# One fused core program, 832 operations: another order on every queue, the same operations

## The chip, the core and the metric

The program runs on one NeuronCore of a Trainium2 chip. Five engines have instruction queues of their own and work through them strictly in order: TensorE (PE in the profile, its weight loads PEld), VectorE (DVE), ScalarE (ACT), GpSimd (POOL) and SyncE (SP, which here issues nearly all DMAs). They wait for one another through semaphores. The metric is the device time of the program in microseconds (us), lower is better. Time before: 160.24 us, the median of 3 runs (159.95 to 160.32).

## The reference

Two independent computations share the core, and their results stand side by side in the output (2048 rows, 576 + 576 columns).

```python
# A: gated long convolution (S = 2048, D = 576, 4 taps)
k_shift = sum over t of k_pad[:, t:t+S, :] * shift_k[:, ks-1-t]
kv = k_shift * v
y  = irfft(rfft(kv padded to 2S) * rfft(ssm_k padded to 2S))[:S]   # per channel
a  = q * (bf16(y) + kv * ssm_D)
# B: linear attention, 32 heads of 18
q, k, v = split(x @ wqkv);  phi(t) = where(t > 0, t + 1, exp(t)) + 1e-6
kv  = einsum("bhsd,bhse->bhde", phi(k), v);  z = sum_s phi(k)
o   = (phi(q) @ kv) / (phi(q) . z + 1e-6)
b   = o @ wo
return concat([a, b], axis=-1)
```

## The kernel before

The kernel first records 832 operations in a list (`Prog.op`): each has the buffers that it reads and writes and the engines that may run it. Nothing in that list says in which order they run. `_issue` reads the order from two tables of numbers at the end of the file. `PLAN` is a list of tokens such as `P391` or `D142`: the letter gives the engine (P TensorE, D VectorE, A ScalarE, G GpSimd, S SyncE), the number the operation. The tokens of one letter, read from left to right, are that engine's queue. `PLACES` gives each buffer its address in SBUF or its bank in PSUM. Where a new buffer lies on an older one, its first writer waits for the older one's last users.

Part A is a Fourier convolution in two steps, since n = 16a + b:

- the taps (L402, `tap`; L236, `tap+` and `tapv`) make kv from k and v on VectorE and GpSimd, in six pieces (three ranges of 192 channels, two halves of b);
- L436 transposes the filter, and L467 (`s1h` for the filter, `s1u` for kv) multiplies by a table over a; ScalarE or VectorE moves each result from PSUM to SBUF as `Ch` or `Cu` (L229 and L231 are the helper's lines for such copies);
- VectorE transposes in blocks of 32 (L506), and L515 (`s2h`, `s2u`) does the 16-point step. There are nine pieces of 64 channels, 0 to 8, for the filter and again for kv. Each piece has four L515 operations, one for each quarter of 32 partitions of TensorE's array; they have consecutive tokens, so P391, P393, P395, P397 are quarters 0 to 3 of the filter's piece 0. Each consists of four matmuls of 32x32;
- for each piece two products (L236, `p1` and `p2`) combine the spectra, `p2` with `X`, a copy whose real and imaginary rows DMAs have swapped; L551 (`i1`) and L576 (`i2`) transform back, and the result is multiplied with q and stored.

Part B projects x (L623 k, L644 q; ScalarE takes the exponential, VectorE makes phi), forms G = x^T phi(k) (L673), then kv and M = kv wo (L708, L770), scales phi(q) with the reciprocal denominators (L236, `pqT`), and multiplies with M (L813, `out`), 16 row groups of two halves each, stored from `ob`.

The first part of x is loaded in two pieces (`x_sb0`), transposed by TensorE (L323) and copied to `xT0`; the other three parts come through transposing loads (L345, L347). While x is on its way, nine matmuls on a constant tile (`cft`, L844) keep TensorE at work. Small loads: `srow` holds the four taps' weights, which ScalarE rearranges to `srt`, a DMA writes to `w_scr`, and another reads back broadcast as `Wj`. A manual dependency (`two`) makes a GpSimd product wait for the VectorE product that stands before it in the table; nothing makes a VectorE product wait for a GpSimd one.

SP's DMAs use eight semaphores in turn, so each DMA is issued only when the one eight places before it has landed.

Of the kernel before, what the change touches and what calls it, by code (L numbers as in the profile page):

```python
# [874 lines left out]
S60 S25 P149 P143 D142 D439 P98 D139 S51 A396 G42 A150 P469 A144 P400 A410 P406 P402 D151 D145 A99 A401 P446 A403
G471 D448 A407 S50 P164 A165 S46 S472 P146 P453 D470 D100 A447 P451 S45 P440 G52 D166 P449 D457 A147 P158 A441 D148
P404 A450 P411 A452 D64 A412 P464 A454 G47 P460 P152 A465 A461 P455 P444 A405 P413 A159 A414 S38 A456 D160 P155
A445 P194 D72 P442 P462 P458 S43 P415 A416 S224 P185 D65 A463 A153 D154 A459 P475 A186 A476 A195 P161 P191 A443
P170 A192 D187 D196 A156 P167 A39 A168 A162 G66 D157 D193 S61 S48 P179 A180 P473 P134 S225 D169 S647 A474 D163 P104
P128 D73 S223 A171 G44 A135 D136 D74 A105 D106 A129 S626 S668 D181 D172 P122 A123 P107 G75 G477 D130 A49 A108 P173  # L880
P113 D124 A114 P125 A126 P182 A183 D109 D80 S646 A174 P119 G67 D127 D115 D184 A120 P131 P101 A132 D121 S62 A102
D133 P110 P116 S226 D81 P176 S17 A111 D112 A117 A177 P188 D103 G82 D118 D175 P217 A189 D178 S625 P220 D83 A218 A219
A221 P488 D190 P480 S63 P486 A489 D68 P230 D231 A481 P197 D232 P490 S667 A487 A198 A199 D76 P237 P233 P492 P202
D234 A491 S547 A493 D238 P478 A203 A479 G69 A204 D77 P482 D239 G78 P200 S253 D235 D236 D70 A483 A201 P484 S254 A485
# [5 lines left out]
S588 P693 G251 P319 S252 G249 D320 P691 A694 P339 P679 A686 D616 A692 P683 A684 A340 P344 P356 A357 P506 D680 P580  # L890
D345 P619 D658 P510 D716 P540 A507 P565 A581 A566 P617 S242 G243 P346 A541 P354 P321 A355 A620 D511 A322 P349 P341
P519 A350 P665 P623 P501 D347 A618 P515 D737 D342 P661 S22 P329 A520 D516 P336 D330 P334 A624 A666 P659 P508 P638
D502 A662 A337 P642 D335 P644 P517 D509 P621 P304 S343 P311 D622 A639 A518 A305 A643 A660 A312 P351 A352 D645 P324
P561 S348 A325 S705 S338 P544 P640 P738 P742 P723 A562 D695 P663 P281 A664 A641 P284 A724 D739 D743 A282 S746 P294
# [60 lines left out]
```

## Time and profile before

| | |
|---|---|
| median of 3 runs | 160.24 us |
| span of the profiled execution, first to last instruction | 158.3 us |
| what lies around the span | 1.9 us (160.24 - 158.3) |
| PE busy | 149.8 us, 95% |
| DVE busy | 141.8 us, 90% |
| ACT busy | 125.1 us, 79% |
| POOL busy | 59.6 us, 38% |
| SP's hardware queue, share of 16 DMA engines | 66.6% |

The profiled execution's own device time is not given beside its span; the 1.9 us around it is taken as the same for both kernels. Busy times are of one execution. The profile counts only instructions that compute as busy, and a matmul's end is modelled. The chain of waits is followed back from the last instruction, so it shows one path among several that are nearly as long.

### The profile page before, as it was taken

Reading aid. Unit: us, or ns where it says so; the run is one execution under the profiler, and the core shown is the slowest. Engines: PE = TensorE matmul, PEld = TensorE weight load, DVE = VectorE, ACT = ScalarE, POOL = GpSimd, SP = SyncE. Lnnn points to the kernel's source line nnn. Section 1 sums busy time; section 2 is a strip of 40 time slices with the busy share of each in tenths; the row PEclk is TensorE's granted clock in tenths of the full one; section 3 lists DMA queues with packets and bytes.
Section 4 is the critical chain, followed back from the end, with each engine's and each line's share of the span. In section 5 each row is a group of like instructions: output and inputs, shape, how many; then the busy total and the mean of one; then the engine's idle time right before and its main releaser. Section 6 shows DMA issues by size and latency. Waiting matters only on the chain.

```text
span 158.3 us, 4158 instructions
## 1 busy us (share of the span) xinstructions
PE 149.8 (95%) x1663; PEld 118.6 (75%) x1663; DVE 141.8 (90%) x170; ACT 125.1 (79%) x229; POOL 59.6 (38%) x53
## 2 busy tenths in 40 slices
PE   6899999999999999999999999999999999999960
PEld 2478885535679888788888887877767799999960
DVE  1547999999999998999999999999989999999690
ACT  4038999999996566467559699999899999998760
POOL 8801310011163554603611999799290000001520
PEclk9999999999999999999999999999999999999997
DMA  5999939999999809965546867881463599405766
GB/s 146 283 384 313 245 79 299 284 187 239 352 384 259 299 15 333 377 270 103 99 131 214 159 149 209 312 288 63 178 232 112 173 331 361 143 4 147 188 181 160
DMA packets 26317, 34.37 MB, mean 217 GB/s; under 512 B 15802, under 2 KB 20923, under 8 KB 25530
## 3 DMA queue, kind: packets, MB, share of 16 engines
q1 hardware_dynamic: 25754, 32.54, 66.6%
q0 software_dynamic: 544, 1.57, 5.6%
q8 instruction: 13, 0.21, 0.7%
q14 instruction: 6, 0.05, 0.1%
HBM read 20.86 MB, written 4.99 MB: 163 GB/s over the span
## 4 chain that ended last, share of the span: by engine, by line
PE 78%; ACT 8%; DVE 6%; DMA 2%; issue 1%; SPq 1%; DVEq 0%; ACTq 0%
PE ps_all L813 13%; PE ps_all L623 12%; PE ps_all L673 12%; PE ps_all L644 11%; PE ps_all L467 8%; PE ps_all L551 8%; PE ps_all L515 5%; ACT sph L229 3%; PE ps_all L576 3%; ACT V L229 3%; DMA x_sb<-in_B_x_dram 2%; PE ps_all L436 2%; DVE Ch L231 2%; ACT yb L229 1%; PE ps_all L708 1%
## 5 line engine op out<-in xcount | busy, mean ns | idle before, releaser
L644 PE MATMUL ps_all<-xT,wq 128*126 128x512 bf16 (+1 forms) x100 | 23.8, 381 | 0.1
L813 PE MATMUL ps_all<-M,pqT 126*128 126x288 bf16 (+1 forms) x160 | 22.5, 287 | 0.0
L623 PE MATMUL ps_all<-wk,xT 128*128 128x288 bf16 x160 | 20.4, 286 | 0.4 <-DVE xT L231 0.4
L402 DVE TENSOR_TENSOR m<-kh,Wj 128x6144 bf16<-128x6144 bf16 x6 | 20.1, 3349 | 0.0
L229 ACT ACTIVATE Cu<-ps_all 128x768 bf16<-128x768 f32 x22 | 17.3, 856 | 3.2 <-PE ps_all L467 3.2
L623 PEld LDWEIGHTS <-xT 128*128 128x128 bf16 x160 | 17.4, 110 | 3.1 <-DVE xT L231 0.6
L236 POOL TENSOR_TENSOR pqT<-pqT,rb 126x1024 bf16<-126x1024 bf16 (+1 forms) x9 | 19.1, 2174 | 1.0 <-DVE v L236 1.0
L813 PEld LDWEIGHTS <-pqT 126*128 126x128 bf16 (+1 forms) x160 | 16.6, 110 | 3.7 <-issue 1.9
L644 PEld LDWEIGHTS <-wq 128*126 128x126 bf16 (+1 forms) x100 | 12.5, 131 | 8.7 <-issue 2.2
L229 ACT ACTIVATE V<-ps_all 128x512 bf16<-128x512 f32 x32 | 17.2, 624 | 1.8 <-PE ps_all L551 1.8
L628 ACT ACTIVATE ek<-ps_all,neg 128x576 bf16<-128x576 f32 x16 | 11.9, 743 | 8.3 <-PE ps_all L623 8.3
L467 PEld LDWEIGHTS <-Gsb 128*128 128x128 bf16 x192 | 16.1, 98 | 2.6 <-issue 1.6
L551 PE MATMUL ps_all<-Esb,sph 128*128 128x128 bf16 x144 | 17.9, 219 | 0.1
L551 PE MATMUL ps_all<-Esb,X 128*128 128x128 bf16 x144 | 17.9, 219 | 0.0
L236 POOL TENSOR_TENSOR m<-m 128x1536 bf16<-128x1536 bf16 x4 | 12.4, 3096 | 13.1 <-DVE m L236 8.9
L673 PE MATMUL ps_all<-pk,x_sb 128*128 128x289 bf16 (+1 forms) x128 | 17.1, 287 | 0.0
L229 ACT ACTIVATE sph<-ps_all 128x512 bf16<-128x512 f32 x30 | 16.6, 608 | 0.2
L229 ACT ACTIVATE Ch<-ps_all 128x768 bf16<-128x768 f32 x19 | 15.2, 853 | 1.0 <-PE ps_all L467 0.8
L229 ACT ACTIVATE spu<-ps_all 128x512 bf16<-128x512 f32 x28 | 15.1, 613 | 0.6 <-PE ps_all L515 0.6
L236 POOL TENSOR_TENSOR q<-yb,q 128x384 bf16<-128x384 bf16 x4 | 3.6, 912 | 29.4 <-DVE yb L231 27.6
L673 PEld LDWEIGHTS <-x_sb 128*128 128x128 bf16 x128 | 12.3, 98 | 2.9
L551 PEld LDWEIGHTS <-sph 128*128 128x128 bf16 x144 | 14.0, 98 | 0.5 <-DVE sph L236 0.2
(96 smaller groups left out, 301.9 us busy)
## 6 DMA issues: line engine op xcount, KB each, us to landing
X<-sph SPq DMA_DIRECT2D x18, 256.0 KB
v<-in_A_v_dram SPq DMA_DIRECT2D x2, 1152.0 KB
out_dram<-ob SPq DMA_DIRECT2D x16, 144.0 KB
q<-in_A_q_dram SPq DMA_DIRECT2D x1, 2304.0 KB
out_dram<-q SPq DMA_DIRECT2D x12, 192.0 KB
rb<-r_scr SPq DMA_DIRECT2D x8, 252.0 KB
x_sb<-in_B_x_dram SPq DMA_DIRECT2D x3, 576.0 KB
kh<-in_A_k_dram SPq DMA_DIRECT2D x1, 1584.0 KB
```

The costliest lines, as they stand in the source:

```text
L229: nc.scalar.activation(out=o, in_=i, func=ACTF.Copy)
L236: return (nc.vector if e == "DVE" else nc.gpsimd).tensor_tensor(out=o, in0=a, in1=b, op=op)
L402: return nc.vector.tensor_tensor(out=m.t[:], in0=i0, in1=i1, op=ALU.mult)
L467: nc.tensor.matmul(ps.t[:, bank, lo - 384 * bank:hi - 384 * bank], lhsT=Gsb.t[:, b, ri, :], rhs=src[:, lo - CC * j:hi - CC * j], start=Tru ...
L515: nc.tensor.matmul(ps.t[32 * j:32 * j + 32, 0, :], lhsT=W2()[32 * kh:32 * kh + 32, :], rhs=ct.t[32 * kh:32 * kh + 32, 8 * j:8 * j + 8], st ...
L551: nc.tensor.matmul(ps.t[:, 0, 128 * c:128 * c + 128], lhsT=src.t[:, 4 * hh + c, :], rhs=Esb.t[:, 32 + wi, :], start=(wi == 0), stop=(wi == 1))
L576: nc.tensor.matmul(ps.t[:, 0, n * j:n * j + n], lhsT=Esb.t[:, 2 * b + ri, :], rhs=V[gi].t[:, 2 * b + ri, :], start=(ri == 0), stop=(ri == 1))
L623: nc.tensor.matmul(ps.t[:, hh, 0:HALF], lhsT=cols(xT.t[0:KT[t], t, :], r), rhs=wk.t[0:KT[t], t, HALF * hh:HALF * hh + HALF], start=(t == 0 ...
L628: P.op("A", lambda e: nc.scalar.activation(out=eb.t[:], in_=ps.t[:, :, 0:HALF], func=ACTF.Exp, bias=neg1.t[:]), rd=[ps, neg1], wr=[eb], na ...
L644: nc.tensor.matmul(ps.t[0:hn, 0, :], lhsT=wq.t[0:KT[t], t, h0:h0 + hn], rhs=xT.t[0:KT[t], t, :], start=(t == 0), stop=(t == 4))
L673: nc.tensor.matmul(ps.t[0:m, 0, 0:n], lhsT=x4[r // 4].t[:, r % 4, :] if t == 4 else x_sb[r // 4].t[:, r % 4, 128 * t:128 * t + 128], rhs=p ...
L813: nc.tensor.matmul(ps.t[:, 0, 0:HALF], lhsT=cols(pqT[r // 8].t[0:kn, c, 512 * (r // 4 % 2):512 * (r // 4 % 2) + 512], r), rhs=M.t[0:kn, c, ...
```

## The change

No operation is added or removed. `PLAN` and `PLACES` hold other numbers: other orders on all five queues, and 83 operations of 832 go to another engine. The diff is those two tables and nothing else; three of the 36 lines of `PLAN` show its kind (the first line, one in the first run of L515, and the last).

```diff
--- before.py
+++ after.py
 PLAN = """
-G0 G6 D830 P831 G10 S28 A15 S16 G222 S26 G12 G14 G5 P30 D27 G57 P32 D33 A29 G9 G7 D31 S54 P36 A37 S53 G1 G2 S21 P34
...
-D408 P140 A434 A468 P431 P425 S41 P137 P391 D432 P395 A426 P393 P397 D399 A141 S58 S24 A392 P409 D398 A394 S40 A138
...
-D762 S769 P772 A773 S763 P770 A771 D774 S775
+D830 P831 G5 G10 S26 S16 G0 G1 G2 D27 G12 P30 D31 S28 S54 S53 G222 G6 G29 P32 A33 P36 D37 P34 P89 D35 A90 D91 S359 S21
...
+P140 A424 P425 A426 D439 S41 A141 P137 A138 P391 A392 D142 S58 P395 P397 G42 S51 D139 S40 D457 S60 G8 P409 A410 G7 A15
...
+A767 P764 A765 D768 P758 A759 S781 P760 A761 D762 P770 A771 P772 A773 S769 P314 S763 A315 D774 S775 S318
```

Three places on which the working rests follow, as the queues stand in the built programs.

**The start.** ScalarE's first rows before: `warm` is an exponential of one element, `x40` a copy of a strip of x, `srt` the rearranged tap weights.

```order
L283 ACT_TABLE_LOAD
L283 ACTIVATE warm_6_76<-neg1_1_57 128x1
L229 ACTIVATE x40_11_87<-x_sb0_5_74 128x2x64
L229 ACTIVATE xT0_13_102<-ps_all 128x256
L628 ACTIVATE ek_19_141<-ps_all,neg1_1_57 128x576
L628 ACTIVATE ek_20_154<-ps_all,neg1_1_57 128x576
L628 ACTIVATE ek_21_174<-ps_all,neg1_1_57 128x576
L229 ACTIVATE hT0_22_177<-ps_all 128x8x128
L229 ACTIVATE hT0_22_177<-ps_all 128x8x64
L229 ACTIVATE Ch_29_228<-ps_all 128x4x96x2 x4
L229 ACTIVATE Ch_33_294<-ps_all 128x4x96x2
L229 ACTIVATE srt_34_298<-srow_31_255 64x36
```

ScalarE's first rows after:

```order
L229 ACT_TABLE_LOAD
L229 ACTIVATE xT0_9_92<-ps_all 128x256
L628 ACTIVATE ek_12_127<-ps_all,neg1_6_76 128x576
L628 ACTIVATE ek_16_146<-ps_all,neg1_6_76 128x576
L229 ACTIVATE srt_17_148<-srow_15_134 64x36
L628 ACTIVATE ek_19_171<-ps_all,neg1_6_76 128x576
L229 ACTIVATE hT0_18_169<-ps_all 128x8x64
L229 ACTIVATE hT1_21_203<-ps_all 128x8x64 x2
L229 ACTIVATE Ch_23_213<-ps_all 128x4x96x2 x6
```

`srt` moved from behind five evictions of `Ch` to before the third exponential; `x40` went to GpSimd, and the large eviction of `hT0` (128x8x128) to VectorE. On SP the rows that follow from it, before:

```order
L222 DMA srow_31_255<-in_A_shift_k_dram 64x36
L222 DMA wq_25_184<-in_B_wqkv_dram 64x576
L222 DMA wq_25_184<-in_B_wqkv_dram 128x4x576
L222 DMA kh0_12_98<-in_A_k_dram 15x1728
L347 DMA_TRANSPOSE xT1_39_356<-in_B_x_dram 128x1x512
L222 DMA kh0_12_98<-in_A_k_dram 112x1728
L222 DMA w_scr<-srt_34_298 64x4x9
L345 DMA_TRANSPOSE xT1_39_356<-in_B_x_dram 128x4x512
L222 DMA kh0_12_98<-in_A_k_dram 128x4608
L222 DMA Wj_44_399<-w_scr 128x2304
L347 DMA_TRANSPOSE xT3_46_425<-in_B_x_dram 128x1x512
```

and after:

```order
L222 DMA kh0_29_296<-in_A_k_dram 15x1728
L222 DMA hs_31_301<-in_A_ssm_k_dram 96x2048
L222 DMA wq_26_244<-in_B_wqkv_dram 128x4x576
L222 DMA w_scr<-srt_17_148 64x4x9
L222 DMA wq_26_244<-in_B_wqkv_dram 64x576
L347 DMA_TRANSPOSE xT1_37_354<-in_B_x_dram 128x1x512
L222 DMA kh0_29_296<-in_A_k_dram 112x1728
L347 DMA_TRANSPOSE xT3_42_383<-in_B_x_dram 128x1x512
L345 DMA_TRANSPOSE xT1_37_354<-in_B_x_dram 128x4x512
L222 DMA kh0_29_296<-in_A_k_dram 128x4608
L222 DMA wv5_10_97<-in_B_wqkv_dram 64x576
L222 DMA Wj_57_506<-w_scr 128x2304
```

`w_scr`, which waits for `srt`, moved ahead of all transposing loads, and `srow` (13th DMA before) is now the 8th. A small load of `kh0` (k with its halo) stands ahead of the two first transposing loads.

**GpSimd's last products**, before (`rb` are the reciprocal denominators, `spu` and `sph` the spectra of kv and of the filter):

```order
L236 TENSOR_TENSOR pqT0_36_332<-pqT0_36_332,rb_137_1442 126x1024
L236 TENSOR_TENSOR pqT0_36_332<-pqT0_36_332,rb_149_1556 126x1024
L236 TENSOR_TENSOR X_82_735<-spu_151_1577,X_82_735 128x2048
L236 TENSOR_TENSOR q_175_2003<-yb_183_2294,q_175_2003 128x2x192
L236 TENSOR_TENSOR q_175_2003<-yb_185_2323,q_175_2003 128x2x192
L236 TENSOR_TENSOR q_175_2003<-yb_184_2303,q_175_2003 128x2x192
L236 TENSOR_TENSOR q_175_2003<-yb_186_2397,q_175_2003 128x2x192
```

and after:

```order
L236 TENSOR_TENSOR pqT0_41_371<-pqT0_41_371,rb_131_1440 126x1024
L236 TENSOR_TENSOR pqT0_41_371<-pqT0_41_371,rb_139_1501 126x1024
L236 TENSOR_TENSOR X_147_1567<-spu_143_1535,X_147_1567 128x2048
L236 TENSOR_TENSOR sph_54_466<-spu_143_1535,sph_54_466 128x2048
L236 TENSOR_TENSOR q_180_2151<-yb_177_2123,q_180_2151 128x4x192
L236 TENSOR_TENSOR q_180_2151<-yb_184_2271,q_180_2151 128x2x192
L236 TENSOR_TENSOR q_180_2151<-yb_186_2388,q_180_2151 128x2x192
```

Both products of piece 3 now stand on GpSimd, one behind the other; before, VectorE made the one into `sph`.

**The end**, on SP before:

```order
L222 DMA out_0_dram<-ob_176_2072 128x576
L222 DMA out_0_dram<-q_175_2003 128x4x192 x2
L222 DMA out_0_dram<-ob_174_2000 128x576
L222 DMA out_0_dram<-q_175_2003 128x4x192 x5
L222 DMA out_0_dram<-ob_161_1718 128x576
L222 DMA out_0_dram<-q_175_2003 128x4x192 x5
```

and after:

```order
L222 DMA out_0_dram<-q_180_2151 128x4x192 x2
L222 DMA out_0_dram<-ob_156_1693 128x576
L222 DMA out_0_dram<-q_180_2151 128x4x192 x4
L222 DMA out_0_dram<-ob_157_1701 128x576
L222 DMA out_0_dram<-q_180_2151 128x4x192 x5
L222 DMA out_0_dram<-ob_175_2042 128x576
```

A store of `ob` now is the very last DMA; the five matmuls that feed its second half (P314) moved from the middle of the last stage to behind the last `i2`.

More of the change, by code (lines that the diff above doesn't have):

```diff
@@ L875 @@
[L875 to L884, printed above, removed]
@@ L890 @@
[L890 to L894, printed above, removed]
@@ new lines @@
+P140 A424 P425 A426 D439 S41 A141 P137 A138 P391 A392 D142 S58 P395 P397 G42 S51 D139 S40 D457 S60 G8 P409 A410 G7 A15
+P393 A394 P143 A144 D145 P149 A150 D448 A396 P98 A99 D100 G13 D151 G57 G52 P146 A398 A147 D148 P404 D405 P406 A407
+P442 A443 P164 P451 A165 D166 P446 P453 P400 S224 A454 A401 A452 P469 D470 S25 D64 A447 P158 P444 P449 A159 D160 A450
+D72 A445 P464 P402 A403 P152 P155 A465 P455 A456 P413 A414 P440 A441 S50 P185 P462 A463 S46 G47 P411 A412 G471 A156
+D157 P458 A459 P191 A192 S45 P415 D65 G66 P460 A461 A416 A153 D154 P194 P161 A162 D163 A195 D196 D193 S472 S48 A186
@@ new lines @@
+P488 P212 A213 D70 D71 A489 S223 P490 A491 S255 P207 D84 G85 S263 P492 A493 A214 P202 A203 D494 D512 A208 D503 A209
+P521 A522 S252 P531 A532 A204 P200 A201 S226 P533 P525 P535 A526 A536 A534 P215 P523 A524 P527 P529 A528 A530 D579
+D537 A216 P205 A206 P614 A615 P610 P604 A605 A611 P210 A211 G262 G260 S244 P600 D256 A601 P687 A688 P689 A690 D264
+P499 A500 D558 P513 D514 P227 D228 D229 P612 A613 P608 D609 P602 A603 P267 D268 G266 P275 A276 P269 P271 S257 G258
+A272 D270 P273 D274 P582 P504 A505 P497 P495 A583 P606 D498 A607 A496 G86 D87 P277 D278 P679 P681 A680 A682 S265 S246
@@ new lines @@
+P685 A686 P344 A345 P339 A340 P691 A692 P693 D616 D658 P683 D684 A694 P319 P356 A357 D320 P506 A507 D637 S242 S250
+P580 A581 P565 P540 S248 P510 D511 P617 A541 P619 A618 P349 A350 A620 P354 D566 D355 P321 D322 P341 A342 S646 S625
+P665 A666 S668 G251 G249 D737 P515 P623 P621 P661 P659 D660 D624 P519 A662 A516 A622 G245 G247 P336 A337 P346 A520
+D347 G243 P334 A335 P329 A330 S626 G627 S589 G628 P517 P561 A562 P644 D716 P642 A643 D518 P638 P501 D502 P508 P351
+D352 A645 P304 A509 D305 A639 P324 A325 P311 A312 S647 S567 P719 D695 P723 D720 P663 A664 P738 P740 D741 P544 A545
@@ new lines @@
+P742 A743 P281 A282 S22 P294 A295 D724 D739 P284 A285 P542 D543 P696 P702 A697 P640 D641 S705 P721 D722 D649 S704 S358
+S747 S343 S338 S588 P538 P331 P286 D648 S547 A539 A703 A332 P289 A287 P717 A290 P563 S667 D669 P698 P744 A699 P559
+A718 A745 D670 P700 A701 D707 P629 S546 P635 A636 P309 S726 S288 S746 P633 A634 P296 A297 P631 S348 A564 A630 P306
+P656 A307 P650 A657 P671 D632 D706 A560 S725 D728 P675 D727 P677 S353 A676 P279 P673 D672 A678 A310 S313 A651 P652
+A674 P710 A653 D749 P586 P584 A587 D711 A585 D590 P316 P708 A317 P735 A280 A736 P654 A655 A709 P714 P731 D748 P712
```

31 lines of the change are left out of this document (13 added, 18 removed), and 32 rows, old and new, of the table PLACES.

## The prediction

> **What bounds the kernel now.** I read the busy shares first, then the busy time by stage.
>
> ```profile
> span 158.3 us, 4158 instructions
> PE 149.8 (95%) x1663; PEld 118.6 (75%) x1663; DVE 141.8 (90%) x170; ACT 125.1 (79%) x229; POOL 59.6 (38%) x53
> ...
> core 0: us, PE busy (x) PEld busy (x) DVE busy (x) ACT busy (x) POOL busy (x), PEclk, DMA share, GB/s
> 8.20:24.20 16.00, 15.55 (x160) 13.11 (x160) 12.85 (x19) 12.89 (x19) 2.98 (x7) 1.00 0.89 250
> 24.20:45.00 20.80, 20.74 (x191) 11.55 (x191) 20.80 (x22) 20.54 (x40) 3.22 (x3) 1.00 1.09 285
> ...
> 105.00:124.40 19.40, 19.40 (x277) 13.33 (x276) 18.17 (x27) 18.31 (x44) 10.58 (x5) 1.00 0.46 172
> 124.40:136.00 11.60, 11.60 (x178) 11.20 (x177) 11.60 (x12) 11.00 (x25) 0.00 (x0) 1.00 0.78 284
> 136.00:151.00 15.00, 14.92 (x223) 14.56 (x221) 13.33 (x21) 12.97 (x29) 3.22 (x4) 1.00 0.42 119
> ```
>
> PE is busy nearly all the time from 8.2 to 151 us, at a granted clock of 1.00. It isn't alone: from 24.2 to 45 DVE (20.80 of 20.80) and ACT (20.54) are full as well, and from 105 to 136 all three nearly are. So an order can gain in three ways only: a shorter start, less PE time for the same matmuls, and a shorter end. Everything it gains on PE must also be kept up with by the engines that empty PSUM. Where I say that something comes at a time "by its queue", I have added the durations that stand ahead of it on its engine in the new order, and looked up when that engine had done the same amount of work before. The sum is made against the profiled execution: 158.3 us of span and 1.9 us around it, which together are the median of 160.24.
>
> **The start.** Next I read the timeline of the first 20 us, and SP's waits.
>
> ```profile
> 3.63 0.31 ACT L229 ACTIVATE x<-x_sb 128x128 bf16<-128x128 bf16 x1 [1.39 <-DMA x_sb<-in_B_x_dram]
> 5.43 1.37 DVE L231 COPY x<-x_sb 128x128 bf16<-128x128 bf16 x1 [4.02 <-DMA x_sb<-in_B_x_dram]
> 8.06 0.49 SPq L222 DMA_DIRECT2D srow<-in_A_shift_k_dram  x1
> 8.20 3.85 PE L623 MATMUL ps_all<-wk,xT 128*128 128x288 bf16 x30 [0.43 <-DVE xT L231]
> 13.08 1.02 ACT L229 ACTIVATE hT<-ps_all 128x1024 bf16<-128x1024 bf16 x1 [0.25 <-PE ps_all L436]
> 14.16 1.48 PE L467 MATMUL ps_all<-hT,Gsb 128*128 128x192 bf16 x16
> 18.95 0.22 ACT L229 ACTIVATE srt<-srow 64x36 bf16<-64x36 bf16 x1
> 19.19 0.69 SPq L222 DMA_DIRECT2D w_scr<-srt  x1
> 19.92 3.63 SPq L345 DMA_TRANSPOSE xT<-in_B_x_dram  x1
> ...
> SPq L222 <- DMA wk<-in_B_wqkv_dram: 0.5, 1, 0.5
> ...
> L231 DVE COPY hT<-ps_all 128x1024 bf16<-128x1024 bf16 x3 | 1.9, 677 | 0.0
> ```
>
> The first k projection (L623) starts at 8.20, after a chain: the piece of x that is needed first is loaded third, its strip copy on DVE takes 1.37 us, and PE, evictions and L623 follow. The two pieces change places (S26 first, S28 third). The piece loaded first landed by 3.63, when ACT copied its strip; so the DVE copy now runs from about 3.6 to 5.0, under the nine matmuls on the constant tile. The other strip is on POOL, behind memsets that are done before it lands at 5.4. From the landing at 5.43 the rest of the chain takes 8.20 - 5.43 - 1.37 = 1.4 us, so evictions would allow L623 at about 6.9. But it needs wk too, and wk is at the same place in SP's queue: SP waited for its landing and issued `srow` at 8.06. Its landing just under 8.0 is the new limit, and I take 0.2 us. Ends: 0, if wk lands later beside other traffic, and 1.3 (8.20 - 6.9), if earlier.
>
> At 14.16 the first L467 waited for the eviction of `hT` on ACT (13.08 + 1.02 = 14.10). This eviction is now DVE's, which takes 0.68 for such a copy (the row below), and ACT and DVE then work on the two halves at once. The wait of some 0.3 goes: 0.3 us, from 0 to 0.5.
>
> SP stood still from 14.26 to 19.19, because `srt` was made on ACT at 18.95 only. It is now made in ACT's slot before the third exponential, near 11.5, once `srow`, now 8th, has landed. All later loads move up by 2 to 3 us. I cost this at 0: no PE row before waits for one of them. What hides them is the work of 24 to 45 us; the transposing loads stay one behind the other on this queue, only earlier.
>
> **L515 on PE.** The chain of waits has 12 of the 15 runs of L515 as steps of their own. Four of them:
>
> ```profile
> 28.82 0.55 PE ps_all L515 x16
> 93.15 0.34 PE ps_all L515 x8
> 105.36 0.90 PE ps_all L515 x24
> 112.42 0.99 PE ps_all L515 x28
> ```
>
> The run at 93.15 holds two operations on different quarters of the array, and takes 0.34. The run at 28.82 (P400 P406 P402 P446, quarters 0, 3, 1, 3) has one quarter twice, and takes 0.55. The run at 112.42 has quarter 2 four times: 0.99. So a run costs about 0.34, and 0.21 more for each time that its commonest quarter is repeated; operations on other quarters cost nothing. Counted from the tokens, before there are 15 runs with 18 repeats: 15 x 0.34 + 18 x 0.21 = 8.9 us. After there are 16 runs with 11 repeats: 5.4 + 2.3 = 7.7 us. PE saves 1.1 us (about 0.5 before 45 us, 0.6 after 93).
>
> [...]
>
> Between 0 and 1.1 I take half, 0.55, since DVE and ACT are full beside it but shed some work themselves:
>
> ```profile
> L231 DVE CAST V<-ps_all 128x512 bf16<-128x512 f32 x4 | 2.7, 683 | 0.1
> L231 DVE CAST spu<-ps_all 128x512 bf16<-128x512 f32 x8 | 5.2, 685 | 1.0 <-PE ps_all L515 1.0
> L236 DVE TENSOR_TENSOR pqT<-pqT,rb 126x1024 bf16<-126x1024 bf16 x1 | 0.7, 684 | 0.0
> L686 DVE TENSOR_SCALAR GT<-ps_all,gcol 128x288 bf16<-128x288 f32 x2 | 0.9, 475 | 0.0
> L231 DVE CAST ob<-ps_all 128x288 bf16<-128x288 f32 x10 | 4.5, 447 | 1.3 <-PE ps_all L813 1.1
> L231 DVE CAST yb<-ps_all 128x384 bf16<-128x384 f32 x6 | 3.3, 553 | 0.3 <-ACT yb L229 0.2
> L231 DVE CAST Ch<-ps_all 128x768 bf16<-128x768 f32 x5 | 4.6, 962 | 0.7 <-ACT Ch L229 0.7
> L236 DVE TENSOR_TENSOR sph<-spu,sph 128x2048 bf16<-128x2048 bf16 x9 | 10.8, 1215 | 0.0
> ```
>
> DVE's net exchange: it gains 4 evictions of V (2.7), 2 of spu (1.4) and one `pqT` product (0.7), together 4.8; it gives up 2 of GT (0.95), 3 of ob (1.3), 3 of yb (1.7), one of Ch (1.0) and one `sph` product (1.2), together 6.1. Three evictions of hT of 512 elements are exchanged for 1024, 768 and 512: 768 elements more, at 677 / 1024 ns each an estimate of 0.5. Net -0.8 us. ACT stands on the other side of nearly all these exchanges and gains less than 0.5 by the same kind of sum. So DVE can follow a PE that is about 1 us faster, but not one that is 2 us faster.
>
> **The product that goes to POOL.** POOL makes a product of 2048 columns in 4.07 us, DVE in 1.22:
>
> ```profile
> 114.30 4.07 POOL L236 TENSOR_TENSOR X<-spu,X 128x2048 bf16<-128x2048 bf16 x1 [2.79 <-DVE spu L231]
> ...
> 118.86 1.22 DVE L236 TENSOR_TENSOR sph<-spu,sph 128x2048 bf16<-128x2048 bf16 x1
> ...
> 126.34 0.39 SPq L222 DMA_DIRECT2D q<-in_A_q_dram  x1
> ...
> L236 POOL TENSOR_TENSOR q<-yb,q 128x384 bf16<-128x384 bf16 x4 | 3.6, 912 | 29.4 <-DVE yb L231 27.6 <-ACT yb L229 1.8
> ```
>
> Two in a row take 8.1 us. At 114.30 POOL had waited 2.79 us, for the last eviction of piece 3 (DVE, its matmuls P621). In the new PE order P621 stands 13 places earlier, and its eviction on ACT ends near 111.5; POOL has then just ended its `pqT` products, which ended at 111.5 before. So the two products run from 111.5 to 119.6. By PE's queue of work, the first L551 of piece 3 comes at about 120.9; DVE's next product, in its queue, at about 120.1. Nothing behind them waits: cost 0, with a slack of 0.5 us towards DVE and 1.3 towards PE.
>
> **The end.**
>
> ```profile
> 149.50 0.62 PE ps_all L813 x5
> ...
> 151.00:158.30 7.30, 2.09 (x26) 1.86 (x23) 3.22 (x7) 2.43 (x6) 0.34 (x1) 0.87 0.69 184
> ...
> 151.89 3.23 SPq L222 DMA_DIRECT2D out_dram<-q  x5
> 152.65 1.25 ACT L229 ACTIVATE yb<-ps_all 128x384 bf16<-128x384 f32 x3 [0.26 <-DVE q L236]
> 153.57 1.03 DVE L236 TENSOR_TENSOR q<-yb,q 128x768 bf16<-128x768 bf16 x2
> ```
>
> After PE's last L576, ACT, DVE and the store of q follow, to 158.3. Five matmuls of L813 (0.62 us, as the row at 149.50) move behind the last L576, where PE has nothing else; the last stage starts 0.6 us sooner. I take 0.4, as ACT and DVE (12.97 and 13.33 of 15.0) leave room there but one more `yb` goes to ACT; ends 0 and 0.6. The store of `ob` behind the last of q costs one more issue, 0.65 us (3.23 / 5), but it moves fewer bytes than a store of q: +0.2, from 0 to 0.65.
>
> **Sum.** -0.2 (x) -0.3 (hT) -0.55 (L515) -0.4 (L813 moved) +0.2 (last store), and +0.15 for waits between engines that no row shows, since the banks and addresses are all new: -1.1 us, 160.24 - 1.1 = 159.1.
>
> **Rivals.**
> 1. PE's savings come through whole: -0.2 -0.5 -1.1 -0.6 = -2.4, 157.8. For it: PE sets the pace in all stages. Against: DVE sheds only 0.8.
> 2. The engines that empty PSUM set the pace. Then L515 and L813 bring nothing, the start brings 0.5, and the last store and new waits take it back: 160.2. For it: the full rows from 24 to 45 and 105 to 136. Against: DVE's load falls by 0.8.
> 3. Slower, at one place: POOL's second product. If POOL starts as late as before (114.30), it ends at 114.3 + 8.1 = 122.4, L551 of piece 3 waits 1.5 us, and DVE, whose own product is due at 120.1, is held 2.3 us if the two can't run side by side. They never do in this trace, so it can't say that they can; but the DVE strip copy at 5.43, with POOL's memsets beside it, took 1.37, and ACT's copy of the same size 0.31. Price: 159.1 + 2.3 = 161.4; DVE's hold is POOL's start + 8.1 - 120.1, so it uses up the gain of 1.1 from a start of 113.1 on. For it: 114.30 is what was measured. Against: the eviction it waited for moves up. [...]
> 4. q comes too late. Its load was issued at 126.34. It now stands behind the store of a row group whose eviction comes, by ACT's queue, at 128.6, so about 2.5 us later. 2304 KB at the 284 GB/s of 124.4 to 136 are 8.3 us: it lands at 137.2, and the first product with q, now on POOL, is due at 137.7. At the 172 GB/s of 105 to 124.4 it would land at 142.6, still in time for DVE's first (142.8 by its queue), but POOL's, twice as wide as the 0.91 us ones, would start 4.9 us late and hold its `yb` buffer, the evictions into it and PE behind them. For that I take its length, 1.8 us: 160.9. For it: the two times are 0.5 us apart. Against: the rate of that stage was the higher one.
>
> **Chances.** Forecast 0.47 (own range 158.2 to 159.9), rival 1 0.12, rival 2 0.14, rival 3 0.18, rival 4 0.09. The 0.2% that a measurement can tell are 0.32 us, so 159.92 to 160.56 is "same". Rivals 3 and 4 are slower, and a quarter of rival 2: 0.30. Most of the rest of rival 2 is same: 0.10. The forecast, rival 1 and the last of rival 2: 0.60. The range leaves out the lower half of rival 1 and the worse half of rival 3: 157.7 to 161.4.
>
> **What would show it.** The first L623 at 8.0; the first L467 near 13.6; `w_scr` issued near 12; runs of L515 of 0.34 where quarters differ; POOL's two large products from about 111.5 to 119.6, with DVE products of 1.22 behind them; L576 ending about 1.3 us before 153.1. I am wrong if DVE shows products of 3 us at 119 to 123, if PE has gaps of over 0.5 us that weren't there, or if SP waits long before q.

## The result, and the profile after

| | before | after |
|---|---|---|
| median of 20 runs (lowest to highest) | 160.21 us (159.86 to 161.93) | 163.15 us (160.72 to 165.92) |
| profiled execution: time, span | 160.24, 158.3 | 162.71, 160.7 |
| mean granted clock of the profiled execution | 0.994 | 0.984 |

The ratio is 1.011, with a 95% interval of 1.008 to 1.014; it leaves out after's ten runs above 162.9, which the comparison takes for disturbed, though no run of the kernel before went above 162, so that here they probably belong to the kernel; with them the medians differ by 1.8%. So the change makes the kernel slower, and it scatters over 5 us, where 18 of the 20 runs of the kernel before lie within 0.7. The forecast was 159.1, the range 157.7 to 161.4.

Head of the page after, with the clock by slices:

```profile
PE 149.5 (93%) x1663; PEld 118.6 (74%) x1663; DVE 139.5 (87%) x167; ACT 124.7 (78%) x231; POOL 61.8 (38%) x54
...
PEclk9999999999999999999999999959999999999997
```

PE is 149.5 us busy as before (149.8); but the clock is down to 0.5 in the slice near 105 us, where the kernel before has full clock. The waits of PE after, and the busy time by stretches (columns as in the prediction's first view):

```profile
PE ps_all L467 <- DVE v L236: 1.6, 1, 1.6
...
PE ps_all L623 <- DMA wk<-in_B_wqkv_dram: 1.4, 1, 1.4
PE ps_all L467 <- ACT Ch L229: 0.8, 1, 0.8
PE ps_all L813 <- DVE M L801: 0.3, 1, 0.3
```

```profile
86.00:96.00 10.00, 10.00 (x117) 8.69 (x115) 9.35 (x11) 9.40 (x15) 6.03 (x4) 1.00 1.03 275
100.86:104.27 3.41, 1.48 (x14) 1.16 (x12) 2.47 (x3) 2.36 (x3) 2.29 (x2) 1.00 0.53 211
104.27:107.68 3.41, 3.41 (x21) 2.68 (x19) 1.83 (x3) 2.38 (x4) 3.41 (x3) 0.50 0.45 178
```

The 1.6 us wait for `v` is new, and in the 3.41 us behind it the clock is 0.50. Where the rest of PE's time went can be counted: for each matmul operation the time from its start to the start of the next, less the usual time of its kind (an L467 takes 0.33, an L813 0.62, and so on). L515 is kept apart and counted with all its time. By stage, in us:

| lost on PE | to 24 us | 24 to 93.7 | 93.7 to 110 | 110 to the end | L515 in all |
|---|---|---|---|---|---|
| before | 1.9 | 0.9 | 0.6 | 0.9 | 9.6 |
| after | 1.9 | 1.1 | 4.2 | 0.8 | 8.1 |

So L515 saves 1.5 us, the start nothing, and 3.6 us go at one place. There the timeline of POOL reads before:

```profile
86.53 1.21 POOL L407 DMA_DIRECT2D m<-m  x1 [6.75 <-DVE m L402]
87.64 6.43 POOL L236 TENSOR_TENSOR pqT<-pqT,rb 126x1024 bf16<-126x1024 bf16 x3
94.12 0.58 POOL L790 MEMSET M<- 64x576 bf16 x1
94.78 3.10 POOL L236 TENSOR_TENSOR m<-m 128x1536 bf16<-128x1536 bf16 x1
97.85 2.12 POOL L236 TENSOR_TENSOR pqT<-pqT,rb 126x1024 bf16<-126x1024 bf16 x1
```

with this time from issue to landing of POOL's own DMA:

```profile
m<-m POOLq DMA_DIRECT2D x1, 768.0 KB, 6.4
```

After, with DVE and PE behind it, and the landing again:

```profile
86.29 1.21 POOL L407 DMA_DIRECT2D m<-m  x1 [7.19 <-DVE m L402]
87.07 4.68 POOL L236 TENSOR_TENSOR pqT<-pqT,rb 126x1024 bf16<-126x1024 bf16 x2
91.81 0.58 POOL L790 MEMSET M<- 64x576 bf16 x1
96.52 2.12 POOL L236 TENSOR_TENSOR pqT<-pqT,rb 126x1024 bf16<-126x1024 bf16 x1 [4.14 <-DMA rb<-r_scr]
98.61 3.10 POOL L236 TENSOR_TENSOR m<-m 128x1536 bf16<-128x1536 bf16 x1
...
101.74 0.96 DVE L236 TENSOR_TENSOR v<-m,v 128x1536 bf16<-128x1536 bf16 x1 [2.15 <-POOL m L236]
...
102.75 0.49 PE L467 MATMUL ps_all<-v,Gsb 128*128 128x192 bf16 x4 [1.63 <-DVE v L236]
103.54 1.90 PE L813 MATMUL ps_all<-M,pqT 126*128 126x288 bf16 x10 [0.30 <-DVE M L801]
```

```profile
m<-m POOLq DMA_DIRECT2D x1, 768.0 KB, 9.6
```

Two kinds of transfers meet here. SP loads `rb`, rows of 1/den (252 KB each), for the products `pqT<-pqT,rb`. POOL issues one DMA of its own that accumulates into `m` (L407, 768 KB), then adds into the same `m` (operation 86, "the sum"); after that DVE multiplies `v` (87) and PE transforms it (L467). In the new order one product on POOL (258, which needs row load 257) stands ahead of the sum, and its row lands at 96.4 only, 8.8 us after its issue at 87.6. Before, the row was issued later, at 92.0, and landed at 95.5. From 86 to 96 the DMA engines are full after the change (1.03, in the row above), and were not before:

```profile
86.00:96.00 10.00, 10.00 (x116) 8.62 (x114) 9.75 (x13) 8.49 (x13) 9.33 (x6) 1.00 0.73 171
```

SP's new order puts the load of `wv` (576 KB, at 42 us before, now at 83.6) and a row load of the other half (244, first needed at 107 us; issued at 93.8 before, now at 86.7) among the rows.

### The profile page after: what moved, and what is told of

Read it like the earlier page. It is cut to its first block, busy times and chain, and to the rows that moved or that the text cites. A ratio compares the mean times of both kernels' runs of the same rounds, so it can differ in the third digit from the quotient of the medians.

```text
span 160.7 us, 4157 instructions
## 1 busy us (share of the span) xinstructions
PE 149.5 (93%) x1663; PEld 118.6 (74%) x1663; DVE 139.5 (87%) x167; ACT 124.7 (78%) x231; POOL 61.8 (38%) x54
## 4 chain that ended last, share of the span: by engine, by line
PE 77%; DMA 9%; DVE 4%; issue 2%; ACT 2%; POOL 2%; SPq 1%; ACTq 0%; DVEq 0%; POOLq 0%
PE ps_all L644 14%; PE ps_all L813 13%; PE ps_all L623 12%; PE ps_all L551 10%; PE ps_all L673 10%; PE ps_all L467 6%; DMA rb<-r_scr 5%; PE ps_all L515 4%; PE ps_all L576 4%; DMA wk<-in_B_wqkv_dram 3%; PE ps_all L436 2%; POOL m L236 2%; SPq L222 1%; ACT yb L229 1%; DVE Ch L231 1%
## 5 line engine op out<-in xcount | busy, mean ns | idle before, releaser
L644 PE MATMUL ps_all<-xT,wq 128*126 128x512 bf16 (+1 forms) x100 | 24.3, 382 | 0.0
L813 PE MATMUL ps_all<-M,pqT 126*128 126x288 bf16 (+1 forms) x160 | 23.4, 293 | 0.3 <-DVE M L801 0.3
L623 PE MATMUL ps_all<-wk,xT 128*128 128x288 bf16 x160 | 20.7, 286 | 1.4 <-DMA wk<-in_B_wqkv_dram 1.4
L623 PEld LDWEIGHTS <-xT 128*128 128x128 bf16 x160 | 17.5, 110 | 4.5 <-issue 1.2
L467 PEld LDWEIGHTS <-Gsb 128*128 128x128 bf16 x192 | 16.9, 101 | 5.0 <-issue 3.5
L813 PEld LDWEIGHTS <-pqT 126*128 126x128 bf16 (+1 forms) x160 | 16.9, 111 | 4.6 <-issue 2.5
L236 POOL TENSOR_TENSOR pqT<-pqT,rb 126x1024 bf16<-126x1024 bf16 (+1 forms) x8 | 17.3, 2237 | 5.3 <-DMA rb<-r_scr 4.1
L229 ACT ACTIVATE V<-ps_all 128x512 bf16<-128x512 f32 x28 | 15.5, 613 | 1.1 <-PE ps_all L551 0.8
L631 DVE SCALAR_TENSOR_TENSOR pk<-ek,ps_all 128x576 bf16<-128x576 bf16 x16 | 11.6, 748 | 3.7 <-ACT ek L628 3.7
L647 ACT ACTIVATE eq<-ps_all,neg 126x512 bf16<-126x512 f32 (+1 forms) x20 | 13.1, 708 | 2.1 <-PE ps_all L644 2.1
L229 ACT ACTIVATE spu<-ps_all 128x512 bf16<-128x512 f32 x26 | 14.4, 611 | 0.0
```

Of the source, the lines that this page charges most:

```text
L229: nc.scalar.activation(out=o, in_=i, func=ACTF.Copy)
L236: return (nc.vector if e == "DVE" else nc.gpsimd).tensor_tensor(out=o, in0=a, in1=b, op=op)
L467: nc.tensor.matmul(ps.t[:, bank, lo - 384 * bank:hi - 384 * bank], lhsT=Gsb.t[:, b, ri, :], rhs=src[:, lo - CC * j:hi - CC * j], start=Tru ...
L623: nc.tensor.matmul(ps.t[:, hh, 0:HALF], lhsT=cols(xT.t[0:KT[t], t, :], r), rhs=wk.t[0:KT[t], t, HALF * hh:HALF * hh + HALF], start=(t == 0 ...
L631: P.op("D", lambda e: nc.vector.scalar_tensor_tensor(out=pk[r // 4].t[:, r % 4, 0:D].rearrange("p (h c) -> p h c", h=2), in0=eb.t[:], scal ...
L644: nc.tensor.matmul(ps.t[0:hn, 0, :], lhsT=wq.t[0:KT[t], t, h0:h0 + hn], rhs=xT.t[0:KT[t], t, :], start=(t == 0), stop=(t == 4))
```

## Experiments

Each edit but that of e3 moves a few tokens of `PLAN`; the number behind the letter is an operation, as in the diff above. What PE "loses" is counted as in the table. The ratios are to runs of the kernel before that were made beside each experiment (medians from 159.96 to 160.08).

**e1_tap_first: POOL's sum ahead of the product again.**

```diff
-S257 G258
-A607 A496 G86 D87
+S257 G86 G258
+A607 A496 D87
```

> The changed kernel with one token moved: on POOL the last sum of the convolution (86, L236 m<-m) stands ahead of the product of pqT with the fifth row load (258) again, as before the change. Theory A (POOL waits 4.1 us for that row load, which lands at 96.36; the sum behind it, DVE's v and PE's L467 come 1.6 us late, and the wait of PE then halves the granted clock for 3.4 us): the waits of 1.63 us and 0.30 us at 102.7 to 103.6 go, the clock stays 1.00 from 97 to 112, PE gets back about 3.9 us: 158.9 us, clearly under the kernel before. Theory B (the clock falls because PE is used more densely, not because it waited): the wait goes, the lower clock stays: 160.8. Theory C (the wait only passes on, to the first L813, which needs the product 258): about 162.

Measured: 161.42 us, 1.009 of before (1.007 to 1.011), four runs from 159.95 to 164.03. None of the theories is right here. In the profiled run (159.95, the fastest of the four) the clock stays 1.00, but PE still waits 1.1 us for `v`. POOL and DVE show why:

```profile
96.00 3.10 POOL L236 TENSOR_TENSOR m<-m 128x1536 bf16<-128x1536 bf16 x1 [3.80 <-DVE kvb L715]
99.06 2.13 POOL L236 TENSOR_TENSOR pqT<-pqT,rb 126x1024 bf16<-126x1024 bf16 x1
...
99.31 2.70 DVE L236 TENSOR_TENSOR v<-m,v 128x1536 bf16<-128x1536 bf16 x1
```

```profile
m<-m POOLq DMA_DIRECT2D x1, 768.0 KB, 9.7
```

POOL's accumulating DMA, issued at 86.1, is 9.7 us under way (second fence), so the sum could not start before about 95.8 although it now stands first. And DVE's `v`, which takes 0.95 alone, takes 2.70 when it meets POOL's product: 1.9 us until that ends at 101.2, and 0.8 after it. The wait of PE is due to this hold: with 0.95 us `v` would have been ready at 100.3, and PE began to wait at 100.9. The late sum counts because it pushes POOL's product onto `v`. This is the hold of rival 3, at another place.

**e2_row_early: row load 257 ahead of wv.**

```diff
-A489 S223 P490
-P271 S257 G258
+A489 S257 S223 P490
+P271 G258
```

> The changed kernel with one token moved: SP issues the row load of 258 ahead of the load of wv (576 KB) instead of five DMAs behind it; POOL's order stays that of the change. Theory A: the row lands at about 89 instead of 96.36, POOL's product starts right after 92.4, the sum of the convolution ends near 97.6 instead of 101.70, no wait of PE, clock 1.00: 158.9 us. If it isn't the landing of the row but POOL's order alone that matters, POOL's sum still ends after 100.5 and the time stays above 161.

Measured: 160.12 us, 1.001 (0.999 to 1.004), ten runs from 159.36 to 162.86. The row now lands 4.5 us after its issue and POOL's product no longer waits for it, but the accumulating DMA takes 11.1 us and the sum waits for that; PE waits 0.5 us for `v`. Most of the loss is gone, not all: 160.1 where 158.9 was expected. The profiled run is the slowest, 162.86, and its waits and busy time show a second source of loss, at the start:

```profile
PE ps_all L623 <- DMA wk<-in_B_wqkv_dram: 2.2, 1, 2.2
```

```profile
7.25:10.66 3.41, 1.25 (x13) 0.95 (x11) 0.71 (x2) 0.00 (x0) 0.00 (x0) 1.00 1.02 340
10.66:14.07 3.41, 3.41 (x16) 2.14 (x15) 0.75 (x1) 0.96 (x2) 0.00 (x0) 0.50 1.05 411
```

There `wk` lands at 9.68 instead of 7.89, PE waits 2.2 us, and again 3.41 us of half clock follow.

**e3_dummy: the wait filled with needless matmuls.** They compute nothing of the result.

```diff
+                    for j in range(16 if (nm, cc, ri, bg) == ("u", 2, 0, 3) else 0):
+                        nc.tensor.matmul(ps.t[:, 0, 0:256], lhsT=Gsb.t[:, j, 0, :],
+                                         rhs=Gsb.t[:, j, :, :].rearrange("p r k -> p (r k)"), start=True, stop=True)
```

> The changed kernel with 16 needless matmuls of 256 columns on TensorE ahead of the L467 that waits at 101.1 to 102.75; they write a bank that the L467 then overwrites, so nothing else changes, and PE still starts that L467 when DVE's v is there. Theory A: the wait costs what it did (1.6 us), but the granted clock stays 1.00 from 97 to 112: 162.7 - 2.1 + 0.15 = 160.8 us. Theory B (density): the clock falls all the same, 162.7 or more.

Measured: 161.56 us, 1.010 (1.008 to 1.012), four runs within 0.7. With PE kept busy the clock is 1.00 from 97 to 112:

```profile
97.00:112.00 15.00, 14.36 (x176) 10.98 (x174) 12.34 (x17) 12.87 (x24) 13.31 (x6) 1.00 0.73 249
```

The median is 1.6 us under the changed kernel's 163.15; by the two profiled runs it is 0.9 (162.71 and 161.79), though `wk` landed 0.7 us later in that of e3. 160.8 was expected. So the lower clock came of the wait, not of denser work.

**e4_before_swap: in the kernel before, POOL's sum behind the product.**

```diff
-G266 S246 P612 G86
-P606 G258 S250 D87
+G266 S246 P612
+P606 G258 G86 S250 D87
```

> The kernel before with POOL's sum of the convolution (86) put behind the product 258, as the change has it; SP's loads stay, so that the row lands at 95.49. Theory A (order and late landing together): the sum ends at 100.7 instead of 97.89, DVE's v 0.8 us later than before, PE waits under 1 us, the clock stays 1.00: 161.0 us. If POOL's order alone makes the loss: about 164.

Measured: 160.59 us, 1.003 (1.000 to 1.006); PE waits 0.6 us for `v`, clock 1.00. POOL's order alone costs about half a microsecond: less than the 1.0 of theory A, and far from the 4 of the other.

**e8_before_wv_late: in the kernel before, wv among the row loads.** S223 moves from 42 us to behind S255 in `PLAN`.

```diff
-P128 D73 S223 A171
-S255 D256
+P128 D73 A171
+S255 S223 D256
```

> The kernel before with only the load of wv moved, from 42.01 to behind the second row load (about 82.5 us). Theory A: POOL's accumulating DMA takes about 9 us instead of 6.4, lands near 95.5, the sum ends near 98.6 instead of 97.89, which DVE's v (99.95) doesn't feel; the fifth row load, which stands behind POOL's products there, is as before: 160.2 to 160.9 us (the upper end if POOL's next product then meets DVE's v and holds it). If the late wv alone made the loss: 163.

Measured: 163.26 us, 1.016 (1.010 to 1.023). My number was wrong and the other one right: late `wv` alone makes as large a loss there, but by another path. I had looked at the fifth row only. The third and fourth rows stood behind `wv` too, and POOL's first product started at 90.89 instead of 87.64:

```profile
90.89 6.30 POOL L236 TENSOR_TENSOR pqT<-pqT,rb 126x1024 bf16<-126x1024 bf16 x3 [2.89 <-PE ps_all L467]
```

The page names an L467 as releaser, but the row of that product (259) landed at 90.71. DVE then waited 1.44 us for this product, and PE in turn for four results of DVE (`GT` 0.7, `v` 0.7, `sph` 0.5, `kvb` 0.2 us). The clock stayed full (0.999 in the mean) and the DMA engines were at 0.77 from 86 to 96. So this run shows that a late `wv` is dear, not that it is dear in the way of the changed kernel.

**e5_wv_early: in the changed kernel, wv issued at 57.8 us.**

```diff
-A489 S223 P490
-S62 D127
+A489 P490
+S62 S223 D127
```

> The changed kernel with one token moved: SP issues the load of wv (576 KB) near 45 us, where the DMA engines are nearly idle in the changed kernel (0.10 of 45 to 56), instead of at 83.62, among the row loads. POOL's order is that of the change. Theory A (the 576 KB among the row loads make both the fifth row load and POOL's own accumulating DMA land late, 9.6 us after its issue instead of 6.4): the accumulating DMA takes about 6.5 us, the row lands by 93, POOL's sum ends near 97.7, DVE's v at about 100, PE has no wait over 0.2 us from 97 to 105: 158.5 us, and the runs scatter less than those of the changed kernel. Rival (the wait comes from POOL's order as such): PE still waits over 0.8 us there, above 160.

Measured: 159.87 us, 0.998 (0.995 to 1.001), twelve runs from 159.22 to 160.94. Scatter and most of the loss are gone, but theory A's numbers don't come: the accumulating DMA takes 8.4 us (6.5 expected), row 257 lands at 95.7 (93 expected), and PE still loses 0.85 us at 100 to 104. Of that 0.2 us are the wait for `v` and 0.3 that for `M`, less than the wait of over 0.8 that the rival asks.

**e9_rows_order: wv early, row 257 ahead of the third and fourth, row 244 behind.**

```diff
-A489 P490 A491 S255
-G262 G260 S244 P600
-P271 S257 G258
-A682 S265 S246
+A489 S257 P490 A491 S255
+G262 G260 P600
+P271 G258
+A682 S265 S244 S246
```

> wv early, and two more tokens moved on SP: the fifth row load (257) ahead of the third and fourth, and the first row load of the other half (244), not needed before 106 us, from between them to behind 265. Theory D (what is late is what the DMA engines carry from 86 to 96, beside POOL's accumulating DMA, and not POOL's order): row 257 lands by 90, the accumulating DMA takes 7 us or less, POOL's product 258 ends by 95, its sum by 98.5, PE has no wait over 0.1 us for DVE's v, 0.5 us less from 97 to 105 than with wv early alone. The start is as there, so 159.4 us in the median. Rival (DVE and POOL themselves set the pace there): PE loses the 0.85 us from 100 to 104 all the same, 159.9.

Measured: 159.35 us, 0.9925 (0.990 to 0.995), seven runs from 158.36 to 161.47. PE loses 0.1 us from 98 to 104, and 258 ends at 94.9, the sum at 98.0. Theory D is right in its outcome; its "7 us or less" is not: the accumulating DMA takes 8.9, but POOL has its product out of the way by then.

**e13_rows_only: the rows put right, wv left among them.** The edit of e9 without its move of S223 (257 ahead of it).

> The changed kernel with the order of the row loads alone put right (257 ahead of wv, 244 behind 265); the load of wv stays among them. If the order of the rows is what matters: PE loses under 0.4 us to waits from 97 to 110 (4.0 in the changed kernel), median 159.4. If wv's 576 KB matter as much (with wv early alone PE still lost 0.85 there): the accumulating DMA takes 10 us or more, POOL's sum ends near 100.5 to 101, PE waits 0.3 to 0.8 us, median 160.1.

Measured: 160.41 us, 1.000 (0.997 to 1.003). The second case: the accumulating DMA takes 11.0 us, PE waits 0.4 us for `v` and 0.3 for `M`; the sum ends at 100.0, half a microsecond earlier than said, in the profiled run, which is the fastest (159.38). So `wv` and the rows both matter, and only the two together bring the place back.

**e10_hs_behind and e14_rows_hs: the first load of hs behind the two small ones**, in e9 and in e13.

```diff
-D91 S359 S21 S18 P95
+D91 S21 S18 S359 P95
```

> As the run before, and the load of the first piece of hs (512 KB, 359) put behind the two small loads, as the kernel before has a smaller order there: SP issues it at about 4.3 instead of 3.41, the load of wk right ahead of it. Theory E (the scatter of the changed kernel at its start comes from this load, which shares the DMA engines with wk's last packets): wk lands at 7.7 to 8.2 instead of up to 9.7, fewer runs above 160.5, the median 0.4 us lower, 159.0. Rival (wk's landing scatters whatever follows it): spread and median as in the run before.

> As the run before, with the first load of hs (359) behind the two small loads as well. Theory E (that load holds up wk's last packets): wk lands by 8.3, the highest runs are lower than in the run before and the spread about half; median 0.3 us lower. Rival: no difference in spread.

Measured: e10 159.01 us, 0.9927 (0.991 to 0.994), five runs within 0.4, where e9 had three of seven above 160.7. e14 160.49 us, 1.0035 (1.002 to 1.005), twelve runs from 159.78 to 160.94, where e13 had four of twelve above 162.2. In both pairs the high runs go, and the median is lower in one only. In the nine profiles with the load of hs right behind `wk` (after, e1, e2, e3, e5, e6, e7, e9, e13) `wk` lands between 7.43 and 9.68, in the three with it further behind (e10, e11, e14) between 8.04 and 8.18: steadier, not earlier.

**e12_before_hs: the same load right behind wk, in the kernel before.**

```diff
-S53 G1 G2 S21 P34
-G11 S359 G3
+S53 G1 G2 S359 S21 P34
+G11 G3
```

> The kernel before with one token moved: SP issues the load of hs (512 KB, 359) right behind that of wk, as the changed kernel does, instead of behind two smaller loads. Theory E (this load shares the DMA engines with wk's last packets): wk lands 0.3 to 1.5 us later than 7.97, differently from run to run; runs from 160.1 to 162, median 160.7 where the kernel before has 160.1. Rival (wk's landing scatters whatever follows it, and the kernel before is steady for another reason): as the kernel before, 160.1 with a spread of 0.5.

Measured: 160.30 us, 1.002 (0.999 to 1.004), from 159.85 to 161.68, beside 159.50 to 160.92 of the kernel before (median 159.97). This settles little: the median rises by 0.3, between the 0.6 of theory E and the 0 of the rival, and the spread is 1.8 us beside 1.4. In the profiled run, the fastest, `wk` lands at 8.13; without the swap it landed at 7.86 to 8.43 (before, e4, e8). So in the changed kernel the high runs go with the load's place, here no effect is shown; what makes the difference stays open.

**e6_end_back: e5 with the last row half of o3 back at 138 us.**

```diff
-S769 P314 S763 A315 D774 S775 S318
-A783 P299 A300 P752
-S283 D569
+S769 S763 D774 S775
+A783 P314 A315 P299 A300 P752
+S283 S318 D569
```

> The run before this one (wv early) with the last row half of o3 (L813 P314, its eviction and its store) put back from the very end to about 138 to 140 us. Forecast of the prediction (the move behind the last L576 saves 0.4, its later store costs 0.2): 0.2 us slower than with wv early alone. Rival, from the traces (from the last L576 to the end before 5.21 us, after 6.06): the move gains PE 0.62 and costs 0.85 at the end, so putting it back is 0.2 us faster.

Measured: 161.02 us, 1.000 (0.996 to 1.004), but its runs spread over 4.4 us and those of e7 over 3.7, so the medians say little. By the traces, from the same operation (P794) to the last L576, PE needs 17.16 us with the move (after, e1, e2, e5) and 17.85 without, 0.69 less. From the last L576 to the last landing it takes 4.45 us without the move (e6), and with it 4.6 to 5.0 in those four, but up to 5.4 in the other seven traces that have it (4.9 in the middle of all eleven). So the move gains 0.69 on PE and costs 0.2 to 1.0 behind it: about 0.2 us to the good, as forecast, with the rival's 0.2 the other way still inside what the traces show.

**e7_head_act and e11_all_three: ACT's eviction 368 behind 387**, in e5 and in e10.

```diff
-S20 A368 P386 A387
+S20 P386 A387 A368
```

> wv early, and one more token moved: ACT's eviction of hT 368 behind the eviction 387 of the first L467 result. In the changed kernel 368 waits 0.77 us for DVE's eviction of the same bank, and holds 387, for which PE waits (the next L467 at 16.07). If that is what uses up the gain of the start, PE's wait at 14.8 to 16.07 falls from about 1.0 to under 0.4 us, and the time is 0.6 us lower than with wv early alone, 157.9; if the wait only moves to the next L436 (needs 368) or to L467 at 16.9, the time is the same.

> As the run before, and ACT's eviction 368 behind 387: PE gains 0.6 us between 14.8 and 16.5, if nothing behind it gives that back: 158.4 us, 1% under the kernel before. Rival (DVE and ACT, full from 24 to 45, take the 0.6 back): as the run before.

Measured: e7 160.56 us, 0.999 (0.994 to 1.003); e11 159.03 us, 0.995 (0.992 to 0.997). PE's wait for ACT is gone in both, but neither time falls to what was expected (157.9 and 158.4). In e11 PE starts the L467 that waited at 15.37, where e10 has it at 16.21, and ends 0.5 us earlier than in e10 (151.06 and 151.53). The median is the same to 0.02 us. In e11's trace the last two stores are issued 0.67 us apart instead of 0.46 and land 3.3 and 3.0 us after issue instead of 3.0 and 2.9, and the span is only 0.1 us shorter; whether the end takes the gain back in each run isn't shown.

Views of e10, the version that is faster than both kernels: span and clock, PE's waits, the busy time by stretches, and POOL's sum in the timeline:

```profile
core 0: 156.8 us, clock 0.990
```

```profile
PE ps_all L467 <- ACT Ch L229: 0.8, 1, 0.8
PE ps_all L623 <- DMA wk<-in_B_wqkv_dram: 0.7, 1, 0.7
```

```profile
86.00:96.00 10.00, 9.99 (x117) 8.66 (x115) 9.32 (x11) 9.43 (x15) 8.78 (x6) 1.00 0.85 225
97.00:104.00 7.00, 6.87 (x74) 5.60 (x73) 6.77 (x10) 6.83 (x13) 4.40 (x3) 1.00 0.65 227
```

```profile
95.36 3.10 POOL L236 TENSOR_TENSOR m<-m 128x1536 bf16<-128x1536 bf16 x1
```

The wait for `v` is gone, the DMA engines are at 0.85 from 86 to 96, and PE loses 0.4 us from 93.7 to 110 (after 4.2), with L515 at 8.1. By the two profiles the changed kernel and e10 are 4.0 us apart (162.71 and 158.68), and this place is 3.8 of them.

## Why the prediction was wrong

- **The step that failed: "All later loads move up by 2 to 3 us. I cost this at 0", with "+0.15 for waits between engines that no row shows".** It was roughly true of the loads that stood between 19 and 41 us: most moved up, more than half of them by 1 to 3 us, and PE lost hardly more from 24 to 93.7 than before (1.1 against 0.9). Later in the same queue `wv` moved 41.6 us down and a row load 7.1 us up, into the one stretch in which SP's rows and POOL's accumulating DMA are both under way, and POOL's sum moved behind a product that needs one of these rows. I looked at neither queue there. In place of 0.15 it cost 3.6 us on PE: 1.9 of waits, the rest by the half clock behind them (3.41 x 0.5 = 1.7). Eleven of the twenty runs of the changed kernel were slower than the profiled one; what they lost isn't traced. e9 and e10, which undo only the order of these loads and of one at the start, take it all back. None of the rivals was it.
- **x pieces, -0.2: right.** The first L623 started at 7.93, when `wk` landed. The worse end of the range, 0, was not safe: in e2 `wk` landed at 9.68, and PE waited 2.2 us.

```profile
7.93 1.26 PE L623 MATMUL ps_all<-wk,xT 128*128 128x288 bf16 x9 [1.37 <-DMA wk<-in_B_wqkv_dram]
...
11.47 0.67 SPq L222 DMA_DIRECT2D w_scr<-srt  x1
...
13.60 1.15 PE L467 MATMUL ps_all<-hT,Gsb 128*128 128x192 bf16 x12
14.59 0.66 PE L436 MATMUL ps_all<-idw,hs 128*128 128x128 bf16 x8
16.07 0.49 PE L467 MATMUL ps_all<-hT,Gsb 128*128 128x192 bf16 x4 [0.82 <-ACT Ch L229]
```

- **hT, -0.3: right where I looked, and lost 2 us later.** The first L467 came at 13.60, as said, and `w_scr` at 11.47. But ACT's next eviction of hT (368) waited 0.77 us for DVE's of the same bank, and held ACT's first eviction of L467's results; PE waited for it at 16.07. The term is 0.
- **L515, -0.55: right in sign, half the size.** PE saved 1.5 us (9.6 to 8.1), more than the 1.1 counted, and e10 shows that it all reaches the end. The two rows below are seven operations each; from its first matmul to the next operation's such a run takes 0.76 us, where the run before with one repeat more took 0.99. Where all quarters differ it took 0.34 to 0.37 (one 0.41). That DVE and ACT, which empty PSUM, would take half of it back was an estimate that no run shows: DVE's busy time fell by 2.3 us (141.8 to 139.5), where the prediction counted 0.8, and ACT's by 0.4 (125.1 to 124.7).

```profile
112.09 0.83 PE L515 MATMUL ps_all<-ct,idw 32*32 32x512 bf16 x28
115.44 0.82 PE L515 MATMUL ps_all<-ct,idw 32*32 32x512 bf16 x28
```

- **L813 moved, -0.4, and the last store, +0.2: about right together** as far as the traces tell (see e6: 0.69 gained on PE, 0.2 to 1.0 lost behind it; the store of `ob` was issued 0.47 us after the last of q).
- **POOL's second product, 0: right**, though both ran 3.2 us late. DVE's next product came 0.9 us after POOL's ended, and was not held. In e10, without the loss before, the two ran from 111.55 to 119.64, as forecast, and DVE's next came 0.3 us later. The hold that rival 3 fears was measured in e1 (DVE's `v` 2.70 us beside POOL's product, 0.95 alone), but not at its place.

```profile
114.68 4.08 POOL L236 TENSOR_TENSOR X<-spu,X 128x2048 bf16<-128x2048 bf16 x1 [1.39 <-ACT spu L229]
118.73 4.07 POOL L236 TENSOR_TENSOR sph<-spu,sph 128x2048 bf16<-128x2048 bf16 x1
...
123.66 1.22 DVE L236 TENSOR_TENSOR sph<-spu,sph 128x2048 bf16<-128x2048 bf16 x1
...
132.72 0.53 SPq L222 DMA_DIRECT2D q<-in_A_q_dram  x1
143.33 1.64 POOL L236 TENSOR_TENSOR q<-yb,q 128x768 bf16<-128x768 bf16 x1 [20.53 <-ACT V L229]
```

- **q too late (rival 4): the delay came, the price didn't.** q was issued at 132.72, 6.4 us later than before, and landed at 143.09; POOL's first product with it started at 143.33. PE is busy for all of 136 to 150.
- **The sum.** That e10 is at 159.0, where 159.1 was forecast, is in part chance: the start brought less and L515 more than written.

## What to carry over

Where an order of queues changes, follow each moved load to the stretch where it lands, and add up what the DMA engines carry there; a load that PE does not wait for can still delay those beside it (POOL's accumulating DMA took 11.0 us with `wv` among the rows, in e13, and 8.9 without, in e9). Take a transfer's time in a trace with its neighbours in that trace: row load 257 took 3.5 us from issue to landing in before and 8.8 in after. Look for the short wait that can cost twice, by the clock that falls behind it (in after 1.6 us of wait, then 3.41 us at a clock of 0.50).

## What the runs showed of the hardware

- **A wait of 1.6 us was followed by half the clock** (after, 104.27 to 107.68; with the wait filled with matmuls, in e3, it was 1.00 from 97 to 112). In after the clock changes at 104.27, 107.68 and 158.88 us: one step of 3.41 us, then fifteen (51.20). It was 0.50 for one step after steps in which PE was busy 1.48 (after) and 1.25 us (e2), and stayed 1.00 after steps with 1.46 (e5, row below), 1.50 (e6) and 1.51 (e3). The wait for `wk` was 2.2 us in e2 and in e5; the clock fell behind it in e2 and not in e5. So neither the length of a wait nor PE's busy time in the step tells the two apart with any margin, and what decides is not shown. The steps start at another moment in each run (one at 5.28 us in after, at 4.95 in e5, at 7.25 in e2). PE had been busy for 43% of the step (1.48 of 3.41 us) when the clock fell in after.

```profile
4.95:8.37 3.42, 1.46 (x22) 1.26 (x21) 1.49 (x3) 0.38 (x1) 0.55 (x2) 1.00 1.01 350
```

- **POOL's accumulating DMA** of 768 KB took 6.4 us in before (with the DMA engines 0.73 busy from 86 to 96), 8.3 in e10 (0.85), 9.6 in after (1.03) and 11.2 in e14, with different loads of SP's queue beside it.
- **DVE's product of 1536 columns** took 0.95 us alone, 2.70 in e1 and 1.92 in e8 beside a POOL product; one of 2048 columns took 1.56 instead of 1.22 where it met POOL's product at 143.33 in after. DVE's `q<-ps_all,q`, which has one input in PSUM, took 0.55 beside a POOL product (before, 147.78) and without one (after, 147.18).
- **The landing of `wk` scattered with what followed it on the queue**: over 2.2 us in nine traces with the 512 KB of hs right behind, over 0.14 in three with two small loads between. In the order of the kernel before it landed at 7.86 to 8.43 in three traces, and with hs right behind at 8.13 (e12), so no rule follows.
